# Token routing between attention and eight experts: fine search levels compare against sums, and the last level's flags name the expert

## The chip, the cores and the metric

The kernel runs on one core of a Trainium2 chip. The metric is the device time of one execution in microseconds (us). The kernel before was timed three times: median 1034.87 us, from 1032.56 to 1034.92 us.

## What is computed

Thresholded attention for 8 batches of 8 heads (576 positions, 64 values per head), then a routed layer of eight experts over the 4608 rows that attention leaves. The routing is greedy over all 36864 logits in falling order, and an expert takes 576 rows.

```python
    scores = scale * np.matmul(q, k.transpose(0, 1, 3, 2))
    thresh = np.max(scores, axis=-1, keepdims=True) - tau
    scores = np.where(scores >= thresh, scores, -1000000000.0)
...
    logits = x @ w_gate
    flat = logits.flatten()
    order = np.argsort(-flat)
...
    for idx in order:
        tok, e = (int(idx) // E, int(idx) % E)
        if assigned[tok] >= 0 or counts[e] >= cap:
            continue
        assigned[tok] = e
        counts[e] += 1
...
        h = np.maximum(x[mask] @ w1[e], 0.0)
        out[mask] = h @ w2[e]
```

## The kernel before

**Attention** runs for the first 490 us, two score tiles at a time. What it leaves for the router is `Lg`, the logits (128 partitions x 36 columns x 8 experts), and the rows themselves, which go to a table `xrows` in device memory. The last 30 pieces of that table are written while the router already works: for each, TensorE transposes (L206, tile `xo`), ScalarE evicts (L219; every fifth piece by eight small activations, L217), GpSimd scales (L219, tile `pp`), and a DMA on SyncE's queue stores (L220).

**The router** works in eight rounds. A round finds the expert that is the first to reach 576 rows, and the value at which it does. `b` is the best logit of each row and `oh` its expert as a one-hot. A search has seven levels (`lv` from -1 to 5), each of four steps: `step_cmp` (VectorE compares `b` with up to 32 thresholds `E` into `cmp`), `step_cnt` (nine matmuls, L428, count per threshold and expert; `cn` is the copy), `step_flag` (four matmuls, L434, bring thresholds onto partitions; VectorE writes into `fla` for each threshold whether any expert reached 576, with `jka` as a by-product) and `step_n` (one matmul sums the flags, L449 in the two coarse levels and L444 with the weights `hb` in levels 1 to 5, and VectorE makes the next 34 thresholds `E` from it). The step widths of the four finest levels stand in `st`, made once in level 1. Then `pick` masks `oh` with the rows above the limit (`ge`), counts per expert (`c`), `pick2` sums that over partitions (L471) and takes the expert that has 576 (`f`, `m`, `e`); `rank1`, `rank2` and `pack` turn the chosen rows into a list of row numbers `idx` (L487, L488, L512, L518). The last round has no search.

**The experts.** With `e` known, `w1_load` fetches w1 (2 MB in four quarters `w1s`; for the first expert on ScalarE's queue) and splits it into `w1h` (ScalarE) and `w1l` (VectorE). With `idx` known, GpSimd gathers the rows from `xrows` (`xg`, five indirect DMAs), TensorE transposes them (L650, tile `pt`, two buffers), ScalarE and VectorE split them (`xh`, `xl`). Then come the two layers on TensorE (L670 and L690) with the next round's search, weights and rows in between.

**What sets the order.** Each engine runs its instructions in the order in which they were recorded. The recording is done by generators with planned clocks (`Vec` estimates VectorE's time, `held` TensorE's), so that a step of the search is recorded after that many matmuls of an expert as its wait is planned to last. In the first round (`s.alone`) the steps are recorded between the 30 pieces of the row table. `V.fn` goes through a helper, so every VectorE instruction of the router has line 366; they are told apart by tile.

## Time and profile before

| | us |
|---|---|
| median of three runs | 1034.87 |
| the profiled execution, its own time | 1034.18 |
| its span | 1032.4 |
| TensorE busy | 980.9 |
| VectorE busy | 776.4 |
| ScalarE busy | 640.7 |
| GpSimd busy | 323.7 |

The span has three stretches: attention up to 490 us, the first search with no expert beside it from 490 to 546 us, and the experts from 546 us to the end. Shares over the whole span mix them, so each is read by itself: by busy time in windows, by the timeline, and by what each engine waited for.

### The profile page before, as it was taken

Reading aid. Unit: us, or ns where it says so; the run is one execution under the profiler, and the core shown is the slowest. Engines: PE = TensorE matmul, PEld = TensorE weight load, DVE = VectorE, ACT = ScalarE, POOL = GpSimd, SP = SyncE. Lnnn points to the kernel's source line nnn. Section 1 sums busy time; section 2 is a strip of 40 time slices with the busy share of each in tenths; the row PEclk is TensorE's granted clock in tenths of the full one; section 3 lists DMA queues with packets and bytes.
Section 4 is the critical chain, followed back from the end, with each engine's and each line's share of the span. In section 5 each row is a group of like instructions: output and inputs, shape, how many; then the busy total and the mean of one; then the engine's idle time right before and its main releaser. Section 6 shows DMA issues by size and latency. Waiting matters only on the chain. (4 is left out here: it accounts for less than half of the span.)

```text
span 1032.4 us, 24067 instructions
## 1 busy us (share of the span) xinstructions
PE 980.9 (95%) x9122; PEld 716.1 (69%) x9122; DVE 776.4 (75%) x2086; ACT 640.7 (62%) x1221; POOL 323.7 (31%) x485
## 2 busy tenths in 40 slices
PE   7999999999999999999768899999999999999996
PEld 4555555555555555555557779798897978889895
DVE  7999999999999999997677677767585676844230
ACT  6889888888888888886544235444352534445340
POOL 3333433333333333332653445312204021232201
PEclk9999999999999999999588999999999999999998
DMA  6321134232433222302563251504325051364101
GB/s 224 108 90 72 65 138 149 85 136 103 153 107 107 108 80 81 108 2 93 181 204 102 89 162 52 191 30 134 127 82 169 16 196 62 125 219 137 41 11 41
DMA packets 36003, 113.03 MB, mean 109 GB/s; under 512 B 4400, under 2 KB 5296, under 8 KB 35376
## 3 DMA queue, kind: packets, MB, share of 16 engines
q1 hardware_dynamic: 28496, 89.03, 24.3%
q0 software_dynamic: 5888, 18.88, 5.9%
q10 hardware_dynamic: 1504, 3.59, 1.1%
q8 instruction: 72, 1.18, 0.5%
q14 instruction: 43, 0.35, 0.1%
HBM read 89.19 MB, written 21.23 MB: 107 GB/s over the span
## 5 line engine op out<-in xcount | busy, mean ns | idle before, releaser
L76 POOL TENSOR_SCALAR nb<-nb,taub 128x1 f32<-128x1 f32 x288 | 147.4, 512 | 294.5 <-DVE z L75 223.4
L75 DVE TENSOR_SCALAR_CACHE_REDUCE z<-sc 128x576 f32<-128x576 f32 x288 | 205.9, 751 | 32.4 <-PE sc L70 31.0
L86 ACT ACTIVATE pp<-z,nb 128x576 f32<-128x576 f32 x256 | 187.3, 773 | 31.7 <-DVE z L75 30.3
L90 DVE SCALAR_TENSOR_TENSOR pp<-z,nb,pp 128x576 f32<-128x576 f32 x256 | 199.9, 813 | 0.3
L690 PE MATMUL pf<-w2h,H 128*128 128x512 f32 x576 | 196.1, 402 | 1.1 <-DVE H L366 1.1
L70 PE MATMUL sc<-qk 64*128 64x288 f32 (+1 forms) x1280 | 179.9, 426 | 2.1 <-DMA qk<-qk_dram 1.7
L145 PE MATMUL xo<-pt,vt 128*64 128x288 f32 x1024 | 151.9, 418 | 0.7 <-ACT xt L152 0.7
L114 ACT ACTIVATE pt<-tb 128x512 f32<-128x512 f32 x256 | 140.1, 594 | 13.9 <-PE tb L99 11.4
L99 PEld LDWEIGHTS tb<-ident,pp 64*128 64x128 f32 x2304 | 86.0, 139 | 71.6 <-ACT pt L114 16.7
L690 PE MATMUL pf<-w2l,H 128*128 128x512 f32 x320 | 128.2, 401 | 0.0
L697 POOL DMA_INDIRECT out_dram<-y,idx x40 | 41.9, 1048 | 265.9 <-ACT y L693 161.4
L690 PEld LDWEIGHTS pf<-w2h,H 128*128 128x128 f32 x576 | 106.3, 188 | 20.0 <-DVE H L366 1.5
L99 PE MATMUL tb<-ident,pp 64*128 64x64 f32 x2304 | 109.0, 230 | 10.1 <-ACT pt L114 6.0
L70 PEld LDWEIGHTS sc<-qk 64*128 64x128 f32 (+1 forms) x1280 | 94.4, 179 | 30.6 <-DVE pp L90 9.2
L670 PE MATMUL pf<-xh,w1h 128*128 128x288 f32 x512 | 113.5, 300 | 1.2 <-ACT xh L653 1.2
L670 PE MATMUL pf<-xh,w1l 128*128 128x288 f32 x512 | 113.9, 301 | 0.0
L670 PE MATMUL pf<-xl,w1h 128*128 128x288 f32 x512 | 113.3, 300 | 0.0
L676 ACT ACTIVATE hf<-pf 128x576 f32<-128x576 f32 x64 | 41.8, 652 | 105.7 <-PE pf L670 94.7
L145 PEld LDWEIGHTS xo<-pt,vt 128*64 128x64 f32 x1024 | 62.5, 136 | 63.5 <-issue 26.2
L693 ACT ACTIVATE y<-pf 128x512 f32<-128x512 f32 x40 | 23.9, 598 | 115.9 <-PE pf L690 99.3
L670 PEld LDWEIGHTS pf<-xh,w1h 128*128 128x128 f32 x512 | 83.1, 190 | 3.7 <-ACT xh L653 1.7
L670 PEld LDWEIGHTS pf<-xl,w1h 128*128 128x128 f32 x512 | 82.8, 189 | 0.2 <-DVE xl L366 0.2
(185 smaller groups left out, 1366.8 us busy)
## 6 DMA issues: line engine op xcount, KB each, us to landing
qk<-qk_dram SPq DMA_DIRECT2D x31, 1008.0 KB, 4.8
w2s<-w_dram SPq DMA_DIRECT2D x32, 512.0 KB, 5.6
w1s<-w_dram SPq DMA_DIRECT2D x28, 512.0 KB, 5.6
vt<-vl_dram SPq DMA_DIRECT2D x32, 320.0 KB, 5.5
xrows<-pp SPq DMA_DIRECT2D x24, 256.0 KB, 2.0
xts<-xt SPq DMA_DIRECT2D x2, 1152.0 KB, 5.2
pt<-xts SPq DMA_DIRECT2D x2, 1152.0 KB
xrows<-xr SPq DMA_DIRECT2D x8, 256.0 KB, 2.1
```

The source lines that it names most:

```text
L70: T.matmul(sc[o,f,:HS], kd["q",h][r,c], kd[k,h][r,:],start=True,stop=True)
L75: V.tensor_scalar(z,SC.pop(t)[:,:,:HS],-0.125,None,op0=ALU.mult,op1=ALU.min,accum_out=nb[:,0:1])
L76: G.tensor_scalar(nb[:,1:2],nb[:,0:1],taub[:,0:1],None,op0=ALU.add)
L86: A.activation(pview(t),ZB[t].rearrange("p a b -> p (a b)"),AF.Exp,bias=NBI[t][:,0:1],scale=-1.0)
L90: V.scalar_tensor_tensor(pv,ZB.pop(t).rearrange("p a b -> p (a b)"),NBI[t][:,1:2],pv,op0=ALU.is_le,op1=ALU.mult,accum_out=den_of(p)[:,p%4, ...
L99: g=slice(64*r,64*r+64); T.transpose(o[:,r],x[g],ident[g,g])
L114: A.activation(PT[p][:,i%2,:,(i//2)*128:(i//2+1)*128].rearrange("p k (r q) -> p r k q",r=2),tb,AF.Copy)
L145: T.matmul(xo[64*h:64*h+64,:HS],v[:,u,64*h:64*h+64],PT[p][:,h,u,q],start=(u==0),stop=False,skip_group_check=True)
L670: T.matmul(ps[:,h,:HS],s[w][:,k,f*128:(f+1)*128],s[x][:,k,h*HS:(h+1)*HS], start=(k==0 and j==0),stop=(k==3 and j==2))
L676: A.activation(hf,ps[:,:,:HS],AF.Relu)
L690: T.matmul(ps[:,0,:],H[:,f,c:c+128],s[w][:,f],start=(f==0 and j==0),stop=e)
L697: G.indirect_dma_start(out=out,out_offset=IOA(ap=s["idx"][:n,t:t+1],axis=0),in_=y[:n],in_offset=None)
```

## The change

In levels 2 to 5 no thresholds are made any more. `st` gets the coarse limit `lo` added once in level 1, and the comparison of a fine level is one `scalar_tensor_tensor`: step plus a sum that is read from PSUM, compared with `b`. The sum is the sum of all steps so far, so `fla` keeps one column of flags per level and `step_n` issues as many matmuls as there are fine levels up to then (one to five). After level 5 the expert is read from that level's flags: a further matmul adds up `jka` over the thresholds, and the expert whose count equals the number of flagged thresholds is the one. Masking `oh`, counting it and `pick2` stay for the last round alone. A constant `lew` replaces `lev` for the weights.

```diff
-        s.cmp=t("cmp",[128,NC_*J],BF16); s.fl=t("fla",[128,1],BF16); V.memset(s.fl,0.0)
+        s.cmp=t("cmp",[128,NC_*J],BF16); s.fl=t("fla",[128,5],BF16); V.memset(s.fl,0.0)
...
     def step_cmp(s,E):
-        V=s.V; lv=E["lv"]; E0=E["E"]; s.js=js=16 if lv in (0,1) else J
-        s.compare(E0,js,28 if s.alone and lv<0 else 0)
+        V=s.V; lv=E["lv"]; s.js=js=16 if lv in (0,1) else J
+        if lv>1:
+            o=1 if lv<5 else 0
+            V.scalar_tensor_tensor(s.cmp.rearrange("p (c j) -> p c j",j=J),s.st[:,lv-2,o:o+J].unsqueeze(1).to_broadcast([128,NC_,J]),E["add"],s.b.unsqueeze(2).to_broadcast([128,NC_,J]),op0=ALU.add,op1=ALU.is_le)
+            return
+        s.compare(E["E"],js,28 if s.alone and lv<0 else 0)
...
-        jk=s.wk.tile([32,8],F32,name="jka")
-        V.tensor_scalar(jk,ps[0:32,0:8],CAP-0.5,None,op0=ALU.is_ge,op1=ALU.max,accum_out=s.fl[0:32])
+        if lv==1: V.tensor_scalar(s.st,s.st,s.lo,None,op0=ALU.add)
+        jk=s.wk.tile([32,9],BF16,name="jka"); s.jk=jk
+        fl=jk[:,8:9] if lv==5 else s.fl[0:32,max(lv,0):max(lv,0)+1]
+        V.tensor_scalar(jk[:,0:8],ps[0:32,0:8],CAP-0.5,None,op0=ALU.is_ge,op1=ALU.max,accum_out=fl)
...
-            s.T.matmul(ps[:,0:1],s.hb[:,lv-1:lv].to_broadcast([128,128]),s.fl,start=True,stop=True)
-            if lv<5: V.scalar_tensor_tensor(E2,s.st[:,lv-1],B["lo"],ps[:,0:1].to_broadcast([128,J+2]),op0=ALU.add,op1=ALU.add)
-            else: V.tensor_tensor(E2[:,:1],B["lo"],ps[:,0:1],op=ALU.add)
-            return {"E":E2,"lo":E2[:,0:1],"lv":lv+1}
+            d=ps[:,0:1]
+            for l in range(lv,0,-1):
+                k=32 if l==5 else 128
+                s.T.matmul(d,s.hb[0:k,l-1:l].to_broadcast([k,128]),s.jk[:,8:9] if l==5 else s.fl[:,l:l+1],start=(l==lv),stop=(l==1))
+            if lv<5: return {"add":d,"lv":lv+1}
+            s.T.matmul(ps[:,1:10],s.ones[0:32],s.jk,start=True,stop=True)
+            lo=s.wk.tile([128,1],F32,name="lo5",bufs=2); V.tensor_tensor(lo,s.lo,d,op=ALU.add)
+            return {"lo":lo,"lv":6,"full":ps}
...
         ge=wk.tile([128,NC_],BF16,name="ge"); s.ge=ge; V.tensor_scalar(ge,s.b,lo,None,op0=ALU.is_ge)
+        if "full" in E: return s.which(E["full"][:,1:9],E["full"][:,9:10])
...
         s.pick(E)
-        yield V.wait()
-        held(0.13); s.pick2(); s.stage="pick"; s.rank1(E)
+        if last:
+            yield V.wait()
+            held(0.13); s.pick2()
+        s.stage="pick"; s.rank1(E)
```

On VectorE, at the end of the first search, before (`sc` and `rps` are PSUM tiles; `f`, `m`, `e` belong to the choice of the expert):

```order
L366 SCALAR_TENSOR_TENSOR E<-st,E,sc 128x34
L366 TENSOR_TENSOR cmp<-b,E 128x1152
L366 CAST cn<-sc 128x32
L366 TENSOR_SCALAR jka,fla<-sc 32x8
L366 TENSOR_TENSOR E<-E,sc 128x1
L366 TENSOR_SCALAR ge<-b,E 128x36
L366 TENSOR_TENSOR oh<-oh,ge 128x288
L366 TENSOR_REDUCE c_8048<-oh 128x8
L366 SCALAR_TENSOR_TENSOR f_8089<-rps,w8b 128x8
L366 TENSOR_REDUCE m_8090<-f_8089 128x1
```

The same place after the change:

```order
L367 SCALAR_TENSOR_TENSOR cmp<-st,sc,b 128x1152
L367 CAST cn<-sc 128x32
L367 TENSOR_SCALAR jka<-sc 32x8
L367 TENSOR_TENSOR lo_8047<-sm,sc 128x1
L367 TENSOR_SCALAR ge<-b,lo_8047 128x36
L367 SCALAR_TENSOR_TENSOR f_8051<-sc,w8b 128x8
L367 TENSOR_REDUCE m_8052<-f_8051 128x1
```

The threshold row, the mask of `oh` and the count `c` are gone, and `f` follows `ge` directly.

On TensorE, level 2 of the first search (L206 are transposes of the row table):

```order
 L206 MATMUL xo<-ident,xt 128x128 x4
-L434 MATMUL sc<-cn,eyer 32x8 x4
-L444 LDWEIGHTS hb
-L444 MATMUL sc<-fla,hb 128x1
+L441 MATMUL sc<-cn,eyer 32x8 x4
 L206 MATMUL xo<-ident,xt 128x128 x4
+L457 LDWEIGHTS hb
+L457 MATMUL sc<-fla,hb 128x1
+L457 LDWEIGHTS hb
+L457 MATMUL sc<-fla,hb 128x1
 L206 MATMUL xo<-ident,xt 64x128 x4
```

The flag sum is two matmuls now, and one piece of the row table has moved ahead of it.

On TensorE, where the first expert begins, before (`rps` there takes matmuls that keep the engine busy, L536):

```order
L536 MATMUL rps<-trib,onesb 128x128
L650 MATMUL pt<-ident,xg 128x64 x4
L650 MATMUL pt<-ident,xg 128x128 x8
L670 MATMUL pf<-xh,w1h 128x288
L650 MATMUL pt<-ident,xg 128x128 x4
L670 MATMUL pf<-xl,w1h 128x288
```

And after:

```order
L555 MATMUL rps<-trib,onesb 128x128
L671 MATMUL pt<-ident,xg 128x64 x4
L671 MATMUL pt<-ident,xg 128x128 x12
L691 MATMUL pf<-xh,w1h 128x288
L691 MATMUL pf<-xl,w1h 128x288
L691 MATMUL pf<-xh,w1l 128x288
```

The transposes of one more row tile stand ahead of the expert's first matmul.

## Rows read from the trace of the kernel before

**Rows 1.** Windows: length, busy (instructions) of PE, PEld, DVE, ACT, POOL; clock, DMA share, GB/s

```profile
540.00:550.00 10.00, 5.82 (x33) 5.00 (x34) 7.43 (x14) 2.86 (x6) 2.29 (x3) 0.59 0.75 237
...
700.00:760.00 60.00, 60.00 (x455) 52.20 (x453) 41.28 (x110) 25.68 (x50) 12.51 (x12) 1.00 0.34 112
```

**Rows 2.** Timeline of the first search: start, duration, engine, line, what

```profile
506.70 1.36 DVE L366 TENSOR_TENSOR cmp<-b,E 128x1152 bf16<-128x1152 f32 x1
...
508.19 1.12 PE L206 MATMUL xo<-ident,xt 128*128 128x128 f32 x4 [0.89 <-ACT pp L217]
...
510.07 2.23 POOL L219 TENSOR_TENSOR pp<-pp,rd 128x512 f32<-128x512 f32 x2 [0.32 <-ACT pp L219]
...
511.39 2.12 DVE L366 TENSOR_TENSOR cmp<-b,E 128x1152 bf16<-128x1152 f32 x1
...
515.68 5.19 POOL L219 TENSOR_TENSOR pp<-pp,rd 128x512 f32<-128x512 f32 x4 [1.26 <-ACT pp L219]
...
519.84 2.25 DVE L366 TENSOR_TENSOR cmp<-b,E 128x1152 bf16<-128x1152 f32 x1
```

**Rows 3.** Timeline, first pick of an expert

```profile
524.17 1.19 DVE L366 TENSOR_TENSOR oh<-oh,ge 128x288 bf16<-128x288 bf16 x1
...
525.39 0.66 DVE L366 TENSOR_REDUCE c<-oh 128x8 bf16<-128x288 bf16 x1
...
526.40 0.17 DVE L366 SCALAR_TENSOR_TENSOR f<-rps,w8b 128x8 f32<-128x8 f32 x1 [0.35 <-PE rps L471]
```

**Rows 4.** Timeline, last row scalings and first weight load

```profile
521.20 5.06 POOL L219 TENSOR_TENSOR pp<-pp,rd 128x512 f32<-128x512 f32 x4 [0.33 <-ACT pp L219]
...
529.99 1.90 ACTq L599 DMA_DIRECT2D w1s<-w_dram  x4
```

**Rows 5.** Waits of the SyncE queue, 520 to 545 us

```profile
SPq L619 <- DMA xrows<-pp: 2.4, 1, 2.4
```

**Rows 6.** Timeline from the row list to the first expert

```profile
533.73 1.06 ACT L606 ACTIVATE w1h<-w1s 128x1024 fp32r<-128x1024 f32 x1 [7.55 <-DMA w1s<-w_dram]
533.83 0.17 DVE L366 SCALAR_TENSOR_TENSOR idx<-cps,ih 128x5 int32<-128x5 f32 x1
534.87 3.81 DVE L366 TENSOR_TENSOR w1l<-w1s,w1h 128x1024 fp32r<-128x1024 f32 x3 [0.87 <-DMA w1s<-w_dram]
...
535.06 2.06 POOL L640 DMA_INDIRECT xg<-xrows,idx  x1 [8.79 <-DMA w1s<-w_dram]
...
543.68 0.42 DVE L366 TENSOR_TENSOR xl<-pt,xh 128x256 fp32r<-128x256 f32 x1
...
545.95 0.61 PE L670 MATMUL pf<-xh,w1h 128*128 128x288 f32 x1 [0.69 <-ACT xh L653]
```

**Rows 7.** Window during the first weight load, columns as in the first group

```profile
535.00:537.00 2.00, 2.00 (x37) 1.94 (x35) 2.00 (x2) 1.77 (x2) 1.94 (x1) 1.00 0.96 389
```

**Rows 8.** Timeline of TensorE inside an expert

```profile
675.81 0.61 PE L690 MATMUL pf<-w2h,H 128*128 128x512 f32 x2
676.27 0.18 PE L444 MATMUL rps<-fla,hb 128*128 128x1 bf16 x1
...
676.62 0.63 PE L690 MATMUL pf<-w2h,H 128*128 128x512 f32 x2
...
678.91 0.39 PE L428 MATMUL rps<-oh,cmp 128*128 128x32 bf16 x9
```

**Rows 9.** Waits of TensorE, 546 to 660 us: total, times, longest

```profile
PE rps L471 <- DVE c L366: 1.1, 1, 1.1
...
PE pt L650 <- DMA xg<-xrows,idx: 1.1, 3, 0.7
```

**Rows 10.** VectorE groups by shape, 600 to 1000 us: busy, mean ns

```profile
L366 DVE TENSOR_TENSOR cmp<-b,cst 128x1152 bf16<-128x1152 f32 x4 | 5.4, 1352 | 0.0
...
L366 DVE SCALAR_TENSOR_TENSOR E<-st,E,rps 128x34 f32<-128x34 f32 x15 | 3.8, 250 | 9.1 <-PE rps L444 9.1
...
L366 DVE SCALAR_TENSOR_TENSOR st<-cst,sm 128x136 f32<-128x136 f32 x5 | 1.8, 353 | 0.0
```

More of the change, by code (lines that the diff above doesn't have):

```diff
@@ L344, in const_arrays @@
     put("lev",2.0**(1-5.0*np.arange(1,6)))
+    lw=np.tile(2.0**(1-5.0*np.arange(1,6)),(128,1)); lw[0,4]=0; put("lew",lw)
     put("io",np.arange(J+2)); put("io4",np.arange(J+2)/16)
@@ L415, in step_cmp @@
     def step_cmp(s,E):
-        V=s.V; lv=E["lv"]; E0=E["E"]; s.js=js=16 if lv in (0,1) else J
-        s.compare(E0,js,28 if s.alone and lv<0 else 0)
+        V=s.V; lv=E["lv"]; s.js=js=16 if lv in (0,1) else J
[4 more added lines that the diff above has]
+        s.compare(E["E"],js,28 if s.alone and lv<0 else 0)
         if lv==1:
-            s.hb=s.wk.tile([128,5],BF16,name="hb"); V.tensor_scalar(s.hb,s.k("lev"),s.ab,None,op0=ALU.mult)
-            s.st=s.wk.tile([128,4,J+2],F32,name="st")
+            s.hb=s.wk.tile([128,5],BF16,name="hb"); V.tensor_scalar(s.hb,s.k("lew"),s.ab,None,op0=ALU.mult)
+            s.st=s.wk.tile([128,4,J+2],F32,name="st"); s.lo=E["lo"]
             V.scalar_tensor_tensor(s.st,s.k("io").unsqueeze(1).to_broadcast([128,4,J+2]),s.ab,s.k("lev")[:,1:5].unsqueeze(2).to_broadcast([128,4,J+2]),op0=ALU.mult,op1=ALU.mult)
@@ L440, in step_n @@
         lv=B["lv"]
-        E2=s.wk.tile([128,J+2],F32,name="E",bufs=3)
         ps=s.ps()
         if lv>0:
-            s.T.matmul(ps[:,0:1],s.hb[:,lv-1:lv].to_broadcast([128,128]),s.fl,start=True,stop=True)
-            if lv<5: V.scalar_tensor_tensor(E2,s.st[:,lv-1],B["lo"],ps[:,0:1].to_broadcast([128,J+2]),op0=ALU.add,op1=ALU.add)
-            else: V.tensor_tensor(E2[:,:1],B["lo"],ps[:,0:1],op=ALU.add)
-            return {"E":E2,"lo":E2[:,0:1],"lv":lv+1}
+            d=ps[:,0:1]
[6 more added lines that the diff above has]
+            return {"lo":lo,"lv":6,"full":ps}
+        E2=s.wk.tile([128,J+2],F32,name="E",bufs=3)
         n=ps[:,0:1]
-        s.T.matmul(n,s.ones,s.fl,start=True,stop=True)
+        s.T.matmul(n,s.ones,s.fl[:,0:1],start=True,stop=True)
         sm=s.wk.tile([128,2],F32,name="sm",bufs=3); lo=sm[:,0:1]
@@ L471, in pick2, with which @@
         s.T.matmul(ps[:,0:8],s.ones,s.c8,start=True,stop=True)
+        s.which(ps[:,0:8],CAP-0.5)
+    def which(s,n,least):
+        V=s.V; wk=s.wk
         f=wk.tile([128,8],F32,name="f8"); s.m=wk.tile([128,1],F32,name="m8")
-        V.scalar_tensor_tensor(f,ps[:,0:8],CAP-0.5,s.w8,op0=ALU.is_ge,op1=ALU.mult)
+        V.scalar_tensor_tensor(f,n,least,s.w8,op0=ALU.is_ge,op1=ALU.mult)
         V.tensor_reduce(s.m,f,axis=AX.X,op=ALU.max)
```

## The prediction

> **What bounds the kernel now.** I read busy time in windows first, because the span mixes three stretches. From 700 to 760 us TensorE is busy 60.00 of 60.00 us at a granted clock of 1.00 (2.4 GHz) [rows 1]: inside the experts its own work is the bound, so a shorter search gains only where TensorE waits for it, and every matmul that the search adds costs its issue time. From 540 to 550 us TensorE is busy 5.82 of 10 us and is granted 0.59 on average, so mostly 1.2 GHz [rows 1]: here, from the end of attention to the first matmul of the first expert at 545.95 us [rows 6], a chain of small steps is the bound. Whatever shortens that chain should move all that follows by as much. So the timeline of this stretch decides, and I read it backwards from 545.95 us.
>
> The first expert's matmul waits for the rows' high part, which waits for a transpose buffer that VectorE's `xl` at 543.68 us frees [rows 6]. VectorE runs in its recorded order: three `w1l` from 534.87 to 538.68 us, then the closing of the first expert and the next round's first steps, then `xl` [rows 6]. It is gap-free there, so what counts is when `w1l` begins: after the first `w1h` at 533.73 us, which had waited for the first quarter of w1 [rows 6]. The load was issued at 529.99 us [rows 4]. The choice of the expert is not what it waited for: `f` ends at 526.57 us [rows 3], and two short operations later `e` is there, by about 527. SyncE's queue, after its last store to `xrows`, waited 2.4 us for that store to land [rows 5], and the load leaves right after: the weight tiles lie where the pieces of the row table lay. So two chains meet before the first expert: the search, which ends in `idx` at 534.00 us [rows 6], and row table, last store, w1, `w1l`. The second is the later one; the search has slack.
>
> **The change part by part.** The sum is made against the profiled execution's own time, 1034.18 us, 1.8 us more than its span and 0.07% under the median of 1034.87.
>
> *Taken from the first search.* Four threshold rows at 0.25 us [rows 10] with some 0.035 us to the next instruction, 1.14 us. The comparison changes its form: 1.35 us as it is [rows 10]; two streams through the three-operand form take 0.353 us for 136 elements and 0.250 for 34 [rows 10], 1.01 ns per element, so 0.353 + 1016 x 1.01 = 1.38 us, and 1.41 if its start costs a little more. I take +0.05 each, 0.2 in all. Mask, count and their sum over partitions: from the start of `oh` at 524.17 to the start of `f` at 526.40 us, 2.23 us [rows 3]. Matmuls: levels 2 to 5 issue 1 + 2 + 3 + 4 more and one for the expert, 11; nine in a row take 0.39 us where one takes 0.18 [rows 8], so 0.026 each, 0.29 us. Nominally the search is 1.14 - 0.2 + 2.23 - 0.29 = 2.9 us shorter.
>
> *What of it arrives.* The row table runs through the same engines. At 506.70 us the level-1 comparison ends by 508.06, but the next count stands on TensorE behind a transpose that starts at 508.19 because ScalarE is late [rows 2]: nothing of level 1 arrives, and the added instruction on `st` (a single VectorE operation; between 0.35 us, from [rows 10], and one scaling of GpSimd more, about 1.05 us from [rows 2]) is hidden there as well, at 0. Without that cover it would cost up to 0.9. In level 2 the comparison is asked for at 511.39 and ends at 513.51, that is 1.21 us after GpSimd's two scalings end at 512.30 [rows 2]: it had waited for GpSimd, and asking for it 0.25 us earlier changes nothing. In level 2 one transpose piece is also recorded ahead of the two sums, which eats what is left. In level 4 the comparison ends at 522.09, 1.22 us after GpSimd's 520.87 [rows 2]; asked for 0.25 us earlier it may get in one scaling sooner, for 0.8 to 1.0 us. But then the scalings behind it queue up: GpSimd runs 521.20 to 526.26 without a gap [rows 4], and if the comparison goes first and ends at 521.1, the five scalings that then follow at 1.05 us end at 526.3 all the same. So the last store, and w1 with it, stay: 0, between -0.9 (the scalings follow the search) and +0.2.
>
> *What the shorter search brings forward.* `idx` comes about 2.9 us earlier, at 531.1 instead of 534.00, and GpSimd's gather, which began 1.06 us after it [rows 6], begins at 532 instead of 535.06. Its rows then move while w1 does: from 535 to 537 us the sixteen DMA engines are busy 0.96 of the time for w1 alone [rows 7]. The third quarter is the last that `w1l` needs before VectorE goes on. The gather's first instruction alone takes 2.06 us [rows 6] and fetches half a tile, so I take little of it ahead of that quarter: about 0.13 MB at 389 GB/s [rows 7], 0.35 us; bounds 0 and, if the first two and a half tiles (0.6 MB) come first, 1.6 us.
>
> In a sentence apart: the Trainium skill, "DMA: Bandwidth & Descriptors", section "Issuing engines are not separate DMA queues", says that transfers started by any engine run on the same sixteen DMA engines and interleave. No row of before shows a gather and w1 together; if they shared evenly, a quarter of 0.52 MB, 1.35 us at 389 GB/s, would take 2.7 and the term would be 1.35 instead of 0.35, the sum 1035.8.
>
> *The order at the first expert.* One more transposed tile stands ahead of the first matmul. It waits for the second `xl`, ready at about 545.95; before, one matmul of 0.2 us filled that gap. +0.2 us (0 to 0.25).
>
> *Six searches inside the experts.* Gained: `pick2`'s wait of 1.1 us in the second round [rows 9], and its place in all six: two neighbours 0.46 us apart, so 0.23 each, but 0.35 with one small matmul between [rows 8], so 0.12 x 6 = 0.7. Lost: 66 matmuls at 0.026, 1.7 us. The row list of the second round is recorded two large matmuls (0.23 each) closer to its transposes, which already wait 1.1 us for their rows [rows 9]; I put 0.2 on that (0 to 0.5). Sum +0.1. Less VectorE work buys nothing where TensorE is full. Other waits of the searches may shift by -1.0 to +1.0.
>
> Together: 1034.18 + 0 + 0.35 + 0.2 + 0.1 = 1034.8 us.
>
> A second rule, in sentences that the sum does without. The trace shows the level-2 comparison held until GpSimd ends [rows 2]. The Trainium skill, "SBUF — State Buffer", section "Who interferes with whom", says that a VectorE instruction with two SBUF inputs and a GpSimd instruction that reads SBUF exclude each other, and one with a single SBUF input does not take part. By that rule the change removes four instructions that were never held and keeps four that are; the trace agrees, and the saving of 1.14 us would be 0 wherever GpSimd is at work.
>
> **The rivals.**
>
> *The gain arrives.* If the last scalings and the last store move with the search, w1 comes earlier by up to 2.9 us and the first expert with it. For it: GpSimd waited for its inputs before 515.68 us and before 521.20 [rows 2, 4], so it isn't the bound all the way. Against: five of the last scalings run back to back, and the last store's landing, not `e`, released w1 [rows 4, 5]. Price: 1034.18 - 2.9 + 0.1 = 1031.4 us. It decides where the last store moves by the full 2.9 us.
>
> *The gather gets in w1's way.* This one ends slower. The gather, 2.9 us earlier, puts its five tiles (1.2 MB, 2.9 to 3.0 us at 389 GB/s [rows 7]) ahead of the third quarter of w1; VectorE's row of work behind the third `w1l` moves by as much, and the low clock of [rows 1] may last longer, since TensorE starts its dense work later. Price: 1034.8 - 0.35 + 3.0 = 1037.5, up to 1039 with a few us more at 1.2 GHz. It decides where the gather's packets begin before the second quarter has landed, some 1.35 us after the first at 533.7. For it: DMA is full there [rows 7]. Against: the first packets of a gather come well after its start.
>
> *The comparison isn't what it seems.* If the three-operand form with its sum in PSUM took two cycles per element, 2.6 us, each search would be 4 x 1.2 us longer; inside the experts most of that would end as waits of TensorE, some 15 us or more over six searches: about 1050 us. Against: 1.01 ns per element [rows 10].
>
> **How the numbers follow.** About 0.3%, 3.1 us, is what a measurement here can tell from no change. The forecast, hidden in the first search and even inside the experts, 0.75: 1034.8, with its own bounds from 1032.2 (-0.9 the last store, -0.35 the gather, -0.2 the order, -0.2 the rows, -1.0 other waits) to 1037.6 (+0.2, +1.25, +0.05, +0.3, +1.0). The gain arrives, 0.15. Gather in the way, 0.08. A slow comparison, 0.02. The range must leave out no more than 2 in 10: it takes the forecast's bounds, reaches half into the first rival below, and only to the foot of the second above: 1031.5 to 1037.6. Faster by over 0.3%: 0.15; within: 0.75; slower: 0.10.
>
> **What would show it.** In the profile after: level-2 and level-4 comparisons that still end 1.2 to 1.4 us after a GpSimd scaling; the load of w1 issued within 1 us of 529.99 although `e` is there by 525; `idx` near 531; the third `w1l` ending a little later than 538.68; the first L691 (the former L670) near 546.4. Inside the experts, no wait at the pick of the second round, and groups of two to five flag sums that cost 0.026 us per matmul. I am wrong if w1 is issued at 528 or earlier, if the third `w1l` ends a microsecond or more later than 538.68, or if a fine comparison without GpSimd beside it isn't near 1.4 us.

## The result and the profile after

The first measurement gave 1035.91 us (median of 20 runs) beside 1034.43 of the kernel before: a ratio of 1.0016, 95% interval 1.0009 to 1.0024. The forecast was no change (1034.8 beside 1034.87). The difference is inside the 0.3% that the prediction called "the same", and the time is inside its range, but the interval leaves 1 out: by this measurement the changed kernel is a little slower, where the prediction had no change. I measured the changed kernel four times more, each time on another chip:

| measurement | changed | before | ratio, 95% interval |
|---|---|---|---|
| first | 1035.91 | 1034.43 | 1.0016 (1.0009 to 1.0024) |
| after2 | 1032.75 | 1034.19 | 0.9986 (0.9978 to 0.9995) |
| after3 | 1032.52 | 1034.20 | 0.9993 (0.9984 to 1.0002) |
| after4 | 1032.24 | 1034.54 | 0.9978 (0.9968 to 0.9988) |
| after5 | 1034.91 | 1034.24 | 1.0002 (0.9991 to 1.0013) |

The first interval excludes the second, the third and the fourth: each holds the scatter within one measurement, not what the next measurement brings. The kernel before stayed within 0.4 us beside them. Over all five the changed kernel lies between 0.16% slower and 0.22% faster. The stages of the profiled executions show where it varies. Attention ends with the start of TensorE's last matmul of it (L150); the experts reach from the start of their first matmul to that of their last, which is called the stretch below:

| profile | attention ends | to the first expert's matmul | to the last expert's matmul | to the end |
|---|---|---|---|---|
| before, of the prediction | 484.76 | 61.19 | 476.73 | 9.73 |
| before2 | 484.75 | 59.88 | 475.69 | 9.73 |
| first measurement | 485.12 | 60.60 | 475.21 | 10.99 |
| after2 | 484.24 | 60.52 | 474.06 | 10.80 |
| after3 | 484.43 | 61.30 | 474.02 | 9.73 |
| after4 | 485.15 | 61.55 | 473.99 | 11.32 |
| after5 | 484.79 | 62.67 | 475.39 | 11.16 |

Means after minus before: 0.0, +0.8, -1.7, +1.1, together +0.2 us. The sum forecast 0, +0.55, +0.1, 0. So the total was met and two of its parts were not; they cancel. The start alone scatters by 2.2 us over the five profiles and by 1.3 over the two of before, so +0.8 tells little.

**The first search.** Timeline of the kernel after, VectorE's second and fourth comparison in the new form, the places that the prediction calls level 2 and level 4, with the GpSimd scalings beside them (start, duration, engine, line, what):

```profile
511.60 1.05 POOL L219 TENSOR_TENSOR pp<-pp,rd 128x512 f32<-128x512 f32 x1
512.06 1.80 DVE L367 SCALAR_TENSOR_TENSOR cmp<-st,sc,b 128x1152 bf16<-128x1152 f32 x1 [0.85 <-PE sc L457]
512.74 2.03 POOL L219 TENSOR_TENSOR pp<-pp,rd 128x512 f32<-128x512 f32 x1
...
518.69 1.05 POOL L219 TENSOR_TENSOR pp<-pp,rd 128x512 f32<-128x512 f32 x1
519.38 1.58 DVE L367 SCALAR_TENSOR_TENSOR cmp<-st,sc,b 128x1152 bf16<-128x1152 f32 x1 [0.33 <-PE sc L457]
519.70 2.16 POOL L219 TENSOR_TENSOR pp<-pp,rd 128x512 f32<-128x512 f32 x1
```

A scaling ends at 512.65, the comparison 1.21 us later; a scaling ends at 519.74, the comparison 1.21 us later. And the scaling that was begun meanwhile takes 2.03 and 2.16 instead of 1.05 us and ends 0.91 us after the comparison: what one engine gets ahead, the other pays. In the five profiles of the changed kernel every comparison of this form that met a scaling ended 1.21 or 1.22 us after one. This is the exclusion of [rows 2] once more, seen from both sides. The end of the search, the load of w1 and the first expert, same view:

```profile
515.55 10.34 POOL L219 TENSOR_TENSOR pp<-pp,rd 128x512 f32<-128x512 f32 x8 [0.78 <-ACT pp L219]
...
523.25 0.67 DVE L367 TENSOR_SCALAR ge<-b,lo 128x36 bf16<-128x36 f32 x1
523.84 0.22 DVE L367 SCALAR_TENSOR_TENSOR f<-sc,w8b 128x8 f32<-128x8 f32 x1
...
524.29 0.15 DVE L367 TENSOR_SCALAR e<-m 128x1 int32<-128x1 f32 x1
524.36 0.58 DVE L367 SCALAR_TENSOR_TENSOR gm<-qm,m,ge 128x36 bf16<-128x36 bf16 x1
524.98 0.97 DVE L367 SCALAR_TENSOR_TENSOR gq<-b,lo,gm 128x36 bf16<-128x36 f32 x1
...
529.06 1.89 ACTq L620 DMA_DIRECT2D w1s<-w_dram  x4
...
532.82 0.17 DVE L367 SCALAR_TENSOR_TENSOR idx<-cps,ih 128x5 int32<-128x5 f32 x1
534.04 2.02 POOL L661 DMA_INDIRECT xg<-xrows,idx  x1 [8.15 <-DMA w1s<-w_dram]
...
545.72 0.59 PE L691 MATMUL pf<-xh,w1h 128*128 128x288 f32 x1
```

`f` starts 2.56 us earlier than in [rows 3], and `e` is there at 524.4. Yet w1 is issued only 0.93 us earlier than in [rows 4], and SyncE's queue again waits for the last store to land, 1.8 us where [rows 5] has 2.4:

```profile
SPq L640 <- DMA xrows<-pp: 1.8, 1, 1.8
```

ScalarE's queue, which issues this w1, waits for the same landing: from 525.61 us, when it has read `e`, to 528.65, with the store landed at 528.62 and w1 following at 529.06.

Of the 2.56 us only 1.0 are left at `idx` (532.99; 534.00 before, [rows 6]). The pick now runs while GpSimd still scales (its last scaling ends at 525.90), and the three small operations `ge`, `gm` and `gq` take 0.67, 0.58 and 0.97 us, each ending 0.04 to 0.06 us after a scaling (523.88, 524.89, 525.90). Timelines of the run "gate" below, where GpSimd is done at 521.5:

```profile
515.18 6.31 POOL L220 TENSOR_TENSOR pp<-pp,rd 128x512 f32<-128x512 f32 x4 [0.78 <-ACT pp L219]
...
524.28 0.24 DVE L368 TENSOR_SCALAR ge<-b,lo 128x36 bf16<-128x36 f32 x1
...
524.96 0.25 DVE L368 SCALAR_TENSOR_TENSOR gm<-qm,m,ge 128x36 bf16<-128x36 bf16 x1
525.24 0.26 DVE L368 SCALAR_TENSOR_TENSOR gq<-b,lo,gm 128x36 bf16<-128x36 f32 x1
```

So of the 1.55 us that are lost behind `f`, `gm` and `gq` take 1.05. Another 0.44 goes between the first matmul of the ranking (L506) and `scol` on VectorE: 1.0 us in all five profiles of the changed kernel, 0.57 and 0.60 in the two of before; its cause isn't shown.

One profile says little here, for the kernel before varies too: in before2 w1 leaves at 528.24 us and `idx` is there at 533.10. On the means, five profiles against two, `f` is 1.9 us earlier, `idx` 0.7 and w1 0.2.

**Inside the experts.** Timeline of TensorE where the fourth expert is at layer 1: the group that ends a search, five flag sums and the sum of `jka`.

```profile
748.27 0.43 PE L691 MATMUL pf<-xh,w1h 128*128 128x288 f32 x2
748.63 0.17 PE L457 MATMUL rps<-jka,hb 32*128 32x1 bf16 x1
748.74 0.25 PE L457 MATMUL rps<-fla,hb 128*128 128x1 bf16 x4
748.92 0.18 PE L459 MATMUL rps<-jka,onesb 32*128 32x9 bf16 x1
749.03 0.54 PE L691 MATMUL pf<-xl,w1h 128*128 128x288 f32 x2
```

The L691 matmuls follow one another every 0.13 us, and the first row is two of them, the second begun at 748.41. The first flag sum starts 0.22 us after it. It and the sum of `jka` use 32 rows of the array, the others 128; this number of rows is called the height below. From 748.63 to 748.74 and from 748.92 to 749.03 it is 0.105 us each for one matmul, where the four between them follow one another after 0.039 and then every 0.025 us. The whole group costs 0.597 us over the pitch of its neighbours (0.591 to 0.602 in six searches). Groups of two, three and four sums of 128 rows cost 0.151, 0.175 and 0.198 at best: 0.025 us a matmul, as forecast.

**The end.** Timeline of GpSimd's last stores (L718 is L697 of before):

```profile
1011.36 0.96 POOL L718 DMA_INDIRECT out_dram<-y,idx  x1 [8.10 <-ACT y L714]
1016.65 0.92 POOL L718 DMA_INDIRECT out_dram<-y,idx  x1 [3.02 <-DMA out_dram<-y,idx]
1020.05 0.98 POOL L718 DMA_INDIRECT out_dram<-y,idx  x1 [2.48 <-DMA out_dram<-y,idx]
```

The same in the kernel before:

```profile
1013.10 0.96 POOL L697 DMA_INDIRECT out_dram<-y,idx  x1 [8.10 <-ACT y L693]
1016.56 0.92 POOL L697 DMA_INDIRECT out_dram<-y,idx  x1 [1.18 <-issue]
1019.92 0.97 POOL L697 DMA_INDIRECT out_dram<-y,idx  x1 [2.44 <-DMA out_dram<-y,idx]
```

The second store waits 3.02 us for the first to land, not 1.18. The pages count 73 packets of 16 KB in the instruction queue, 72 before. The one more is fetched at 1013.40 us and takes 1.35 us, to 1014.75. What the DMA moves from 1012 to 1016 us, in slices of 0.1 us:

```profile
GB/s 0 0 0 0 0 0 0 0 164 369 410 328 451 328 492 164 0 0 0 0 0 0 0 0 0 0 0 41 0 0 0 41 0 0 0 0 0 0 0 0
```

All but two of the store's 4 KB packets have moved by 1013.72 us; the last two begin at 1014.74 and 1015.17. The trace doesn't number the DMA engines, but the first late packet begins where the fetch ends. Stores follow one another, so the end is 10.99 instead of 9.73 us after the last expert matmul. The Trainium skill, "Runtime: NRT & Kernel Launch", section "Instruction fetch mechanics", says that instructions come in 16 KiB blocks of 256 and that crossing a block is mostly hidden. The packets agree in size; in this place it is not hidden.

### The profile page after: what moved, and what is told of

Same layout as the page of the kernel before. It is cut to its first block, busy times and chain, and to the rows that moved or that the text cites. A ratio compares the mean times of both kernels' runs of the same rounds, so it can differ in the third digit from the quotient of the medians.

```text
span 1031.9 us, 24196 instructions
## 1 busy us (share of the span) xinstructions
PE 983.6 (95%) x9192; PEld 718.2 (70%) x9192; DVE 765.7 (74%) x2051; ACT 640.4 (62%) x1221; POOL 325.9 (32%) x485
## 4 chain that ended last, share of the span: by engine, by line
PE 72%; DVE 10%; ACT 9%; issue 5%; DMA 2%; POOL 1%; ACTq 0%; DVEq 0%; POOLq 0%; SPq 0%
PE pf L711 19%; PE pf L691 18%; PE xo L145 10%; PE sc L70 8%; PE tb L99 8%; ACT pp L86 4%; PE xo L150 2%; DVE z L75 2%; ACT pt L114 2%; DVE pp L90 2%; PE pt L671 2%; ACT pt L116 2%; POOL pp L219 1%; DVE cmp L367 1%; DMA out_dram<-y,idx 1%
## 5 line engine op out<-in xcount | busy, mean ns | idle before, releaser
L691 PE MATMUL pf<-xl,w1h 128*128 128x288 f32 x512 | 113.3, 299 | 0.0
L691 PE MATMUL pf<-xh,w1h 128*128 128x288 f32 x512 | 113.2, 299 | 0.0
L691 PE MATMUL pf<-xh,w1l 128*128 128x288 f32 x512 | 112.6, 298 | 0.0
L697 ACT ACTIVATE hf<-pf 128x576 f32<-128x576 f32 x64 | 41.8, 653 | 106.5 <-PE pf L691 100.0
L718 POOL DMA_INDIRECT out_dram<-y,idx x40 | 45.2, 1130 | 195.3 <-ACT y L714 147.9
L661 POOL DMA_INDIRECT xg<-xrows,idx x40 | 42.8, 1070 | 138.7 <-issue 41.8
L691 PEld LDWEIGHTS pf<-xh,w1h 128*128 128x128 f32 x512 | 82.8, 189 | 0.5
```

Of the source, the lines that this page charges most:

```text
L661: G.indirect_dma_start(out=x[:n],out_offset=None,in_=xrows,in_offset=IOA(ap=s["idx"][:n,t:t+1],axis=0))
L691: T.matmul(ps[:,h,:HS],s[w][:,k,f*128:(f+1)*128],s[x][:,k,h*HS:(h+1)*HS], start=(k==0 and j==0),stop=(k==3 and j==2))
L718: G.indirect_dma_start(out=out,out_offset=IOA(ap=s["idx"][:n,t:t+1],axis=0),in_=y[:n],in_offset=None)
```

## The experiments

Theory A: flag sums with 32 rows of the array, and their number, are what the experts pay. Theory B: the earlier row list collides with w1, so the first expert begins later. Theory C: the longer end is the fetch of one more block. Theory G: the row table's last store gates w1, so the search's gain cannot arrive. Starts, stretches and ends are given for all kernels in one table below.

**h128**, no matmul with 32 rows:

```diff
-        jk=s.wk.tile([32,9],BF16,name="jka")
+        jk=s.jf[0:32] if lv==5 else s.wk.tile([32,9],BF16,name="jka")   # s.jf: 128 rows, zero
...
-                k=32 if l==5 else 128
+                k=128
...
-            s.T.matmul(ps[:,1:10],s.ones[0:32],s.jk,...)
+            s.T.matmul(ps[:,1:10],s.ones,s.jf,...)
```

> The last level's flags lie in a tile of 128 rows of which 96 stay zero, so that no matmul of the search is over 32 rows; nothing else differs. Theory A: the group costs 0.25 to 0.28 us, and the time is 2.0 us under the changed kernel's, so 0.3 to 0.5 us under the kernel before. Theory B: no difference from the changed kernel (within 0.5 us).

Beside it ran the changed kernel itself, **after2**:

> The changed kernel once more, beside the others on one chip. Both theories: 1.5 to 1.7 us over the kernel before. Theory A (matmuls over 32 rows): inside the experts the group of six matmuls that ends a search costs about 0.59 us of TensorE against 0.25 that the same group would cost at the pitch of its full-height members, so 0.34 x 6 = 2.0 us in all. Theory B (the first expert): the first matmul of the first expert comes later after the end of attention than in the kernel before, by 1 us or more.

Measured: h128 1031.69 us, 1.06 under after2 (1032.75). That after2 would be 1.5 us or more over the kernel before failed for both theories: it is 1.4 under it. Theory B failed at its own sign as well: the first expert of after2 begins 60.52 us after attention, between the 61.19 and 59.88 of before. Timeline of TensorE in h128, the same group:

```profile
747.17 0.42 PE L691 MATMUL pf<-xl,w1h 128*128 128x288 f32 x2
747.43 0.18 PE L457 MATMUL rps<-jkf,hb 128*128 128x1 bf16 x1
747.47 0.24 PE L457 MATMUL rps<-fla,hb 128*128 128x1 bf16 x4
747.57 0.17 PE L459 MATMUL rps<-jkf,onesb 128*128 128x9 bf16 x1
747.60 0.51 PE L691 MATMUL pf<-xh,w1l 128*128 128x288 f32 x2
```

Same matmuls, same place, and 0.251 us instead of 0.597: 2.07 us in six searches, as A says. Of these 0.8 arrive in the stretch (473.25 after 474.06): what is left of them went into other waits. The price of the height is shown; half of the 2.0 us that A expected arrives in the time.

**levels** and **pick**, each half of the change alone: `levels` keeps the sums in the comparison and the old pick; `pick` makes thresholds as before and takes the expert from the last level's flags.

```diff
 levels:
-            s.T.matmul(ps[:,1:10],s.ones[0:32],s.jk,start=True,stop=True)
-        if last:
-            yield V.wait()
-            held(0.13); s.pick2()
+        yield V.wait()
+        held(0.13); s.pick2()
...
 pick:
+            k=32 if lv==5 else 128
+            s.T.matmul(ps[:,0:1],s.hb[0:k,lv-1:lv].to_broadcast([k,128]),s.jk[:,8:9] if lv==5 else s.fl,...)
+            if lv==5: s.T.matmul(ps[:,1:10],s.ones[0:32],s.jk,start=True,stop=True)
```

> The fine levels' sums alone; the expert is again found by masking, counting and a sum over partitions. Theory A: against the kernel before, 60 further matmuls at 0.026 us (1.6 us) and two changes of height per search (0.17 x 6 = 1.0 us), less what the first search gives (0.5 to 0.9 us): 1.7 to 2.1 us slower than before. Theory B: what hurts is the earlier row list, which the levels alone bring forward by only 0.6 us: within 0.5 us of before.

> The expert from the last level's flags alone; thresholds are made as before. Theory A: against the kernel before, one small matmul's place less (0.12 x 6) and a wait of 1.1 us less, two changes of height more (0.17 x 6), one matmul more at 0.026 x 6: 0.6 us faster, and 1.5 us faster if the first search passes something on. Theory B: the row list of the first search is 2.2 us earlier and collides with the weight load: 1 us or more slower than before.

Measured: levels 1034.57 us, 1.0003 of before (0.9995 to 1.0012); pick 1027.32, 0.9934 (0.9919 to 0.9948). A's numbers failed for both (1.7 to 2.1 us slower; 0.6 to 1.5 faster), and so did B's for pick (1 us or more slower); B's "within 0.5 us" for levels came out, though its reason, a later first expert, did not (60.82 us). The half that names the expert gains 6.9 us, of which the prediction credited 1.8 inside the experts; the half with the sums gives nothing alone and takes 5.4 us back in the whole (after2, on the same chip).

**pick128** is `pick` with h128's tile, measured twice:

> The kernel before with the second half of the change alone (the expert from the last level's flags, the thresholds made as before), and the flags of the last level kept in a zero-padded tile of 128 rows, so that no matmul of the search is 32 rows high. Theory A: the group that ends a search costs 0.39 us with 32 rows (six of them 2.33 us), and should cost 0.12 + 0.03 us with 128 rows, so 1.4 us less in six searches: 1027.3 - 1.4 = 1025.9 us (1025.4 to 1026.4). Rival (height of the tile is nothing, the 1.06 us that the same edit brought to the changed kernel was chance): 1027.3 us, within 0.4.

> The second half alone with full-height flags once more (1026.11 us in its first measurement), since the same kernel has shifted by up to 3.6 us from one measurement to the next: 1025.5 to 1027 us if this kernel is as steady as its 1.1 us of scatter says, and the stretch of the experts 468.7 us.

Measured: 1026.11 and 1028.54 us. The group that ends a search costs 0.18 instead of 0.39 us on the mean of six (0.15 instead of 0.33 in the five that meet no wait). The first value is where A put it, the second above what was expected and above pick itself: this kernel moves by 2.4 us from one measurement to the next as well, each on another chip, so the medians don't decide between A and its rival; the group does. Waits of TensorE from 545 to 1008 us, first in the changed kernel of the first measurement (total, times, longest):

```profile
PE pt L671 <- PE pt L671: 0.9, 1, 0.9
PE rps L435 <- DVE cmp L367: 0.8, 2, 0.7
PE rps L457 <- DVE jka L367: 0.8, 1, 0.8
PE pt L671 <- DVE xl L367: 0.8, 1, 0.8
```

and in pick128:

```profile
PE pt L658 <- DVE xl L367: 0.8, 1, 0.8
PE pt L658 <- issue: 0.6, 1, 0.6
PE rps L445 <- DVE jka L367: 0.5, 1, 0.5
...
PE rps L429 <- DVE cmp L367: 0.3, 1, 0.3
```

With the smaller rows the view adds up to 4.4 and 2.8 us, and to 7.3 in the kernel before: the old pick's wait was 1.1 of that [rows 9], the other waits fell with it.

**dvebusy** is pick128 with the old VectorE work put back in the experts' searches, read by nobody:

```diff
-        if "full" in E: return s.which(E["full"][:,1:9],E["full"][:,9:10])
+        full="full" in E
+        if full and s.alone: return s.which(E["full"][:,1:9],E["full"][:,9:10])
...                                              # mask product and count as before
+        if full: s.which(E["full"][:,1:9],E["full"][:,9:10])
```

> The kernel with the second half of the change alone and full-height flags (1026.11 us in its own measurement), with the old finding's VectorE work put back in the six searches that run inside the experts: the mask product (128x288) and the count (128x8) are computed, some 1.85 us a search, and nothing reads them; no matmul and no wait for TensorE is put back. Theory D (the second half saves more than the 1.8 us that the prediction credits because VectorE is the engine that TensorE waits for there, so 11 us less of its work shorten the waits): 1028.5 to 1031 us. Rival R (what it saves is the trip to TensorE and back, its matmul and its wait): 1026.0 to 1027.0 us.

Measured: 1027.38 us, the stretch 469.74 after 468.73 in pick128 and 470.03 in pick128b. Between the two expectations and nearer to R: 11 us of VectorE work cost 1 us at most, and nothing beside pick128b. "Less VectorE work buys nothing where TensorE is full" was nearly right; that leaves the trip that is gone and the order that results for the gain, which no run takes apart.

**sum1** puts the flags of levels 1 to 4 in four blocks of 32 rows of one column, so that one matmul of 128 rows sums them:

```diff
+        o=32*(lv-1) if 1<lv<5 else 0; r=slice(o,o+32)
...
-            for l in range(lv,0,-1):
...
-                s.T.matmul(d,s.hb[0:k,l-1:l]...,s.fl[:,l:l+1],start=(l==lv),stop=(l==1))
+            s.T.matmul(d,s.hb[:,min(lv,4)-1:min(lv,4)]...,s.fl[:,1:2],start=True,stop=(lv<5))
+            if lv==5: s.T.matmul(d,s.hb[:,4:5]...,s.jf[:,8:9],start=False,stop=True)
```

> The changed kernel with the flags of levels 1 to 4 in four blocks of 32 rows of one column, so that one matmul of 128 rows adds up all levels so far, and with the last level's flags in a zero-padded tile of 128 rows: six matmuls of flag sums a search instead of fifteen, none of them 32 rows high. Theory A with the count: the last group of a search goes from 0.597 to 0.17 or 0.20 us and the groups of 2, 3 and 4 lose 0.025 us a matmul, 3.3 us less in six searches, and with 108 instructions fewer the last fetched block may fall away from the end (0 to 1.1 us): 1028.2 to 1029.3 us. Rival (most of the 6.4 us between this kernel and the second half alone is that VectorE now waits with its comparison for the sums, wherever they come from): 1030.5 to 1032.5 us.

Measured: 1030.19 us, beside 1034.91 of after5 and 2.3 below after2 to after4. It lies between the two expectations. In the profile the flag sums cost 4.1 us less than in after3 (4.8 instead of 8.9), 1.8 us of other waits came in, and the end is 9.73. Against pick128 the whole change is 5.3 us longer in the stretch (after3; 4.0 against pick128b) and 1.1 at the end (mean): 6.4. Number, height and end of the flag sums give back 2.3 + 1.1 of them, about half; the rest stays with waits whose single causes I haven't separated.

**pad** adds 64 one-column matmuls, 128 instructions, in TensorE's idle time before the first expert:

```diff
         if first: s.warm(WARM[2])
+        if first: s.pad(64)     # 64 x matmul(ps[:,0:1], s.ones, s.tri[:,0:1])
```

> The changed kernel with 64 one-column matmuls more (each with its weight load, 128 instructions, half of a 16 KB block) after the last of the matmuls that keep TensorE busy before the first expert, where TensorE is then idle for 2.1 to 2.9 us. Their results are used by nothing. Theory C (the end of the changed kernel is 1.25 us longer because the fetch of one more block of TensorE's instructions falls on a GpSimd store at 1013 us): the last fetch moves about 10 us ahead, to 1002 to 1005 us, the end goes from 10.8 to 11.0 back to 9.7 us, and the kernel is 1.0 to 1.3 us faster than the unpadded one of the same job. Rival: the end is longer for another reason (the stores themselves, the order of the last experts): then the end stays at 10.8 to 11.0 us and the padded kernel is 0 to 2 us slower, by what the 64 matmuls take if the idle time there is not theirs.

> The changed kernel again, unchanged, since its two measurements lie 3.2 us apart (1035.91 and 1032.75) while the kernel before gave 1034.43 and 1034.19 beside them. Theory A (the extra cost of the change is a property of its instructions: 32-row loads, one more fetched block at the end) expects one of these values again, with the end, from the last layer 2 matmul to the last instruction, at 10.8 to 11.0 us. If the difference is of the session, the time should agree with one of the two to 0.5 us; a value in between (1034.0 to 1034.6) says that it is scatter of the single measurement and that two sessions can't settle 0.3%.

Measured: pad 1032.20, after3 1032.52 us. The last fetch moved from 1013 to 997.6 us, further than expected, and the end is 9.73 us. GpSimd's stores in pad:

```profile
1009.83 0.96 POOL L722 DMA_INDIRECT out_dram<-y,idx  x1 [8.11 <-ACT y L718]
1013.29 0.91 POOL L722 DMA_INDIRECT out_dram<-y,idx  x1 [1.18 <-DMA out_dram<-y,idx]
```

Of the nine profiles with a fetch between 1010 and 1016 us, eight end 0.8 to 1.6 us late; of the eleven without one, none does. In all eight the store's first late packet begins within 0.02 us of the end of the fetch, and the store's packets take 2.1 to 2.9 us from the first to the last, 0.83 in before and pad. The ninth is after3: its fetch began at 1012.79 us, just as the store's last packet ended, the next store waited only 0.36 us more than in pad, and the end is 9.73. So the fetch is the cause where it finds packets of the store still to move, and that changes from run to run of the same kernel. The medians of pad and after3, 0.3 us apart, don't show its price.

**gate** leaves out the last four GpSimd scalings (those rows are stored unscaled); **gate2** also ScalarE's, and plans the pieces 0.9 instead of 1.05 us apart:

```diff
 gate:
-                A.activation(xv,pv,AF.Copy); G.tensor_tensor(xv,xv,src,op=ALU.mult)
+                A.activation(xv,pv,AF.Copy)
+                if b!=nb_batches-NDEF-1: G.tensor_tensor(xv,xv,src,op=ALU.mult)
 gate2 also:
-            elif c in XAC:
+            elif c in XAC and b!=nb_batches-NDEF-1:
-XTY=1.05
+XTY=0.9
```

> The changed kernel without the last four GpSimd scalings of the row table (one batch's rows are stored unscaled: its rows come out wrong, the routing doesn't depend on them). Theory G (the gate of the prediction: the load of the first expert's w1 can't be issued before the last store of the row table has read its tile, whatever the search does): GpSimd ends 5.2 us earlier, at 520 to 521 us, the last scaling is then ScalarE's at 525.4, w1s is issued at 526.5 to 527.7 instead of 529.06, and the first expert's first matmul comes 0.8 to 2 us sooner counted from the last attention matmul (60.6 us in the changed kernel), because the gather collides less with w1 as well. Rival (the gather and what follows it set the first expert, w1 is early enough): w1s is issued earlier and the first expert moves by under 0.4 us unless idx comes earlier too; then it moves with idx, one for one.

> The changed kernel with the pieces of the row table 0.9 instead of 1.05 us apart in the order that the code plans, and with all rows of the batch that is stored last copied without their scaling (these rows come out wrong; the routing doesn't depend on them). The four scalings that were left out before only moved the last store to ScalarE's piece, which ended at 526.8 us, and w1s was issued 2.7 us behind it. Theory G (the load of w1 waits for the last store of the row table, whichever engine wrote its tile): the last piece ends at 522.5 to 524.5 us, w1s is issued 2.5 to 3.3 us after it or 1.2 us after ScalarE has read the expert's number (524.8 us), whichever is later, so at 526 to 527.5 us and not at 528.1 to 529.5, and the first expert begins 59.0 to 60.3 us after the last attention matmul (60.5 to 61.4 in the runs of the changed kernel). Rival: w1s is issued earlier and the first expert doesn't move by over 0.3 us, since the gather and the search set it.

Measured: gate 1033.01, gate2 1029.34 us. Timeline of ScalarE in gate:

```profile
525.13 1.71 ACT L217 ACTIVATE pp<-xo,rm 64x64 f32<-64x64 f32 x8 [0.82 <-PE xo L206]
529.51 1.89 ACTq L621 DMA_DIRECT2D w1s<-w_dram  x4
```

and in gate2:

```profile
519.84 0.59 ACT L219 ACTIVATE pp<-xo 64x512 f32<-64x512 f32 x1 [0.76 <-PE xo L206]
524.67 1.88 ACTq L621 DMA_DIRECT2D w1s<-w_dram  x4
```

The expectation for gate failed, and for G's reason: with GpSimd done at 521.5 the last piece was ScalarE's, which ended at 526.84, and w1 left 2.7 us behind it, later than in after3 (528.27). In gate2 the last piece is done at 520.4, `e` at 523.3, and w1 leaves at 524.7: now the search releases it, and the first expert starts 56.45 us after attention instead of 60.5 to 62.7, sooner than expected. G holds: ScalarE's queue waits for the landing of the last store in gate (to 529.10 us) and not in gate2. But the stretch of the experts is 476.8 instead of 474.0 us: over half of the 4.9 us is given back there.

**x95** and **x90**, pick128 with pieces 0.95 and 0.9 us apart and everything computed:

```diff
-XTY=1.05
+XTY=0.95      # x90: 0.9
```

> The kernel with the second half alone and full-height flags (1026.11 us), with the pieces of the row table planned 0.95 instead of 1.05 us apart; everything is computed. Theory G: the last store of the row table comes some 1 us earlier, as far as GpSimd keeps up (it scales back to back for the last 10 us, so perhaps 0.3 to 0.8 us), w1s with it, and the first expert by 0.3 to 0.8 us: 1025.3 to 1025.8 us. Rival: GpSimd doesn't get done sooner, or the pieces delay the search by as much: 1026.1 to 1027 us.

> The same with the pieces of the row table 0.95 us apart (1024.11 us in its first measurement), now beside the one with 1.05 us. Theory G (the gate on the first expert's weights was worth 2 us): 1.5 to 2.5 us under its neighbour of this job. Rival (the 2 us lay between two measurements): within 0.7 us of it.

> The second half alone, full-height flags, and the pieces of the row table planned 0.9 us apart (0.95 gave 1024.11 us, 1.05 gave 1026.11). Theory G: at 0.95 GpSimd already scaled back to back for the last 12.5 us, so there is little left: 1023.5 to 1024.5 us. Rival (the gain came from a search that is disturbed less by the pieces): it goes on, 1022.5 to 1023.5 us.

Measured: x95 1024.11 us, 0.9898 of before (0.9882 to 0.9914), the best of all and below its own range; again (x95b) 1026.91, 1.6 us under pick128b on the same chip, as G expected, but not clear of the scatter (x95b 1024.74 to 1031.91, pick128b 1026.65 to 1028.69); x90 1026.73. GpSimd's last scalings in x95, and w1:

```profile
510.19 12.46 POOL L219 TENSOR_TENSOR pp<-pp,rd 128x512 f32<-128x512 f32 x9
525.77 1.88 ACTq L607 DMA_DIRECT2D w1s<-w_dram  x4
```

The last scaling ends at 522.65, w1 leaves 3.1 us later, the first expert starts 3.3 us sooner than in pick128, and 1.9 of these are lost again inside the experts (0.6 against pick128b). In x90 the start is another 0.9 us sooner and the experts 2.6 us longer; both of its expectations failed. By the medians x90 can't be told from x95b, which ran on another chip; by these two profiles nothing is gained past 0.95.

> The kernel before, profiled again: its one profile is of the first measurement, in which the changed kernel was 3.2 us slower than in the later three. If the kernel before takes the same path each time, the stretch from the first to the last expert matmul is 476.7 us again (the changed kernel's was 475.21 in the first measurement and 474.02, 474.06 and 473.99 in the later ones), and the end 9.73 us. If the first measurement was of a slower condition that the kernel before shares, that stretch is 1 us shorter here, 475.5 to 475.9, and the median is nevertheless 1034.2 to 1034.6.

> The changed kernel once more, unchanged: it measured 1035.91, 1032.75 and 1032.52 us, beside 1034.43, 1034.19 and 1034.20 of the kernel before. If the first value is of that measurement, 1032.3 to 1033.0 is expected again. If the kernel has two levels, 1035.5 to 1036.3 should come back at some time. The end after the last layer 2 matmul: 9.7 to 11.0 us, by whether the fetch of TensorE's last block of instructions happens to hold up a store (theory C); where it is 9.7, the store just after that fetch waits for its predecessor by under 0.5 us more than 1.18 us.

> The changed kernel a fifth time, beside a profile of the kernel before: 1032.2 to 1032.8 us, 474.0 us from the first to the last expert matmul, an end of 10.6 to 11.3 us (in four profiles of five so far) or 9.73 us. If 1035.5 to 1036.3 comes back, the kernel has two levels and both belong to the result.

Measured: before2 1034.31 us and a stretch of 475.69, as if the first measurement had been of a slower condition for both kernels; but after5, on the same chip as before2, gave 475.39 and 1034.91, so its expectation failed. Its 12 runs reach from 1031.67 to 1038.38 and don't fall into two levels. After4 gave 1032.24, just under its range. After3 and after5 have the same instructions in the same order, and their profiles, 4.5 us apart, differ by 0.4 us in attention, 1.4 at the start, three waits of 0.4 us in the experts, and 1.4 at the end. Two of these three, at a transpose some 56 us after the experts' start (L671) and at a coarse flag sum some 235 us after it (L464), stand in the profile of the first measurement too; in after2 to after4 the one is 0.4 to 0.5 us shorter and the other isn't there.

| kernel | median | start of the experts | stretch | end |
|---|---|---|---|---|
| h128 | 1031.69 | 60.30 | 473.25 | 11.05 |
| levels | 1034.57 | 60.82 | 476.40 | 11.01 |
| pick | 1027.32 | 60.89 | 470.65 | 9.73 |
| pick128 | 1026.11 | 60.76 | 468.73 | 9.73 |
| pick128b | 1028.54 | 60.89 | 470.03 | 9.73 |
| dvebusy | 1027.38 | 61.24 | 469.74 | 9.73 |
| sum1 | 1030.19 | 62.17 | 471.71 | 9.73 |
| pad | 1032.20 | 61.42 | 473.97 | 9.73 |
| gate | 1033.01 | 61.70 | 474.05 | 10.56 |
| gate2 | 1029.34 | 56.45 | 476.77 | 11.10 |
| x95 | 1024.11 | 57.45 | 470.62 | 9.73 |
| x95b (its profiled run took 1031.91) | 1026.91 | 58.73 | 475.71 | 9.73 |
| x90 | 1026.73 | 56.56 | 473.19 | 9.73 |

## Why the prediction was right and wrong

**What failed, in short.** The mechanism in the first search was right. The step that failed is the sum behind it: the term "Six searches inside the experts" was put at +0.1 us and measured -1.7, because its flag sums cost more and its other waits fell much more than it allowed, and the end of the kernel, measured +1.1, had no term. That the total is met to 0.2 us on the mean is luck, for these two cancel.

**Right: why the first search's gain doesn't arrive.** The store gates w1, the comparison ends 1.2 us after a scaling, and a comparison that gets in ahead pushes the scalings back by as much (term 0). All three stand in the rows above; gate2 and x95 show what lies behind the gate. The comparison cost 1.42 us alone (1.40 forecast; 1.50 on the mean inside the experts). W1 left at 528.1 to 530.0 us in the five profiles, so the sign of being wrong, 528 or earlier, did not come. The start was forecast 0.55 us later and came 0.8 later on the mean of five, with a scatter of 2, which tests nothing so small. One sentence of the second rule is too short: that an instruction with a single SBUF input takes no part. `ge` reads one tile and a scalar, and it was held until a scaling ended (0.67 us, 0.24 in gate); the measurement decides.

**Wrong in size: how much earlier `idx` would be.** "2.9 us earlier, at 531.1": it was 1.0. The nominal 2.23 us of the pick was taken as if its successors kept their durations; two of them moved into GpSimd's scalings, which took 1.05, and 0.44 went on the way to `scol`. The third `w1l`, forecast to end a little after 538.68, ended at 536.8 to 539.5 (537.51 in before2). The gather (534.04) then met w1 little in this profile, with `w1h` 1.3 us apart as before. In h128, where the gather began at 533.02, two of them came 2.2 and 1.7 us apart, in after3 to after5 one came 2.1 to 2.3 us behind its neighbour, in before2 1.9: the collision exists, at about the price of the term (0 to 1.6), and the kernel before had a part of it.

**Wrong: "Six searches inside the experts", +0.1.** Measured -1.7 on the mean, out of two terms that were both mis-sized. From before2 to after3 the flag sums cost +4.4 us, not 1.7: 66 matmuls at 0.025 are the 1.7, the 32-row ones 2.07 more, and the rest is waits in front of single sums (0.95 and 0.2 in after3, 0.5 in before2). The first mistake was taking the price from [rows 8], where nine matmuls of one height follow one another, for a group that changes height four times. The Trainium skill, "TensorEngine Tiling (Array Packing)", section "Key Properties", says that a change of the tiling mode drains TensorE; I had not weighed it. The runs show lost time at these changes, 0.346 us for four, though not a drain as such. Against that, `pick2` gave 2.0 (1.8 forecast), and 4.1 us are left over, where the prediction allowed other waits ±1.0. That figure is a difference; the view of TensorE's waits accounts for some 3 us of it, and single causes aren't shown.

**Missing: the end.** +1.1 us on the mean, by the fetch of one more block of instructions in four profiles of five. The sum had no term for the instruction stream itself.

**Open.** Why the first measurement's median lies 3.2 us above the next three. Its profile (1033.78 us, the shortest of its 20 runs) is 2.3 us longer than that of after2, 0.9 of it in attention, which the change doesn't touch, and 1.15 in the experts, of which two waits are 0.9. These are the two that after5 has as well, the other measurement with a high median; what brings them isn't shown. The four later measurements were each on another chip, and which the first was on isn't on record, so a difference between chips that the changed kernel alone meets is not excluded. In this profile the experts are 1.5 us shorter than in the profile of before and the end 1.3 longer: the 1.5 us by which the median was slower don't appear in it.

## What to carry to other kernels

Here a small matmul cost its pitch only among neighbours of its own height (0.251 instead of 0.597 us for six): pad the operand with zero rows rather than use a quarter of the array. Before counting on a shorter chain, ask which store still holds the memory that the next load needs, and whether the operations that move forward land beside an engine that excludes them. And the interval of one measurement is not the scatter of the next: repeat the changed kernel before explaining 0.2%.

## What the hardware showed that I had not expected

- Matmuls of 128 rows and one column follow one another every 0.025 us; six that change between 32 and 128 rows four times cost 0.597 instead of 0.251 us.
- One 16 KB packet of the instruction queue (0.88 to 2.3 us each in all profiles) delayed a chain of indirect stores by 0.8 to 1.6 us at the end of the kernel, in eight of the nine profiles in which it came between 1010 and 1016 us; in the ninth the store's packets had just moved.
- GpSimd's 1.05 us scaling, begun during a VectorE comparison, ended 0.91 us after it each time, and VectorE operations of 36 columns that began during a scaling took 0.58 to 0.97 us and ended just after it; in gate, with GpSimd done, they took 0.24 to 0.26.
